# Seventy short moves in a pinned issue order: attention and early gate/up of a transformer block on one Trainium2 core

## The chip, the cores and the metric

The kernel runs on one core of one Trainium2 chip. The metric is the device time of one execution in microseconds, as a median over several executions. A core has five engines that run side by side, each through its own list of instructions in the order in which they were issued: PE (matrix unit), DVE (vector), ACT (scalar), POOL (GpSimd) and SP, which here only issues DMA transfers. They wait for each other by semaphores.

## The reference

A pre-norm block: linear attention, then a gated feed-forward layer, with 2048 tokens and width 1024.

```python
# x (1, 2048, 1024), wqkv (1024, 3072), wo (1024, 1024); 32 heads of 32; F = 3584
q, k, v = split(layernorm(x) @ wqkv)
phi = lambda t: where(t > 0, t + 1, exp(t)) + 1e-6
kv = einsum("bhsd,bhse->bhde", phi(k), v);  z = sum over s of phi(k)
o = (phi(q) @ kv) / (phi(q) . z + 1e-6)
h = x + o @ wo
n = layernorm(h)
gate = n @ W_gate;  gate = gate * (gate > 0);  up = n @ W_up
h2 = h + (gate * up) @ W_down
```

## The kernel before

Its large products run by the seven-product scheme of Strassen in Winograd's form: DVE forms sums of blocks of both operands, PE makes seven products of half the size instead of eight, and the results are combined in PSUM banks and by copies. Three banks matter: A (two of them), D (one) and E (two).

```python
def strassen(pool, work, mm, fin, sbufs=3, late=False, copies={}):
    ...
    def snap(v, nm, bank=A):              # a partial sum is copied out of its bank by ACT (L203)
        ...
        copies[nm, v] = nc.scalar.copy(out=snaps[nm, v], in_=bank[v][:])

    def m2(v):
        d = pool.tile([P, NW], FP32, tag="D", bufs=1, name="Dq")
        mm(d, 2, v, True)
        fin(0, 0, v, d, snaps["m1", v])
    for v in range(2):                    # product 1 -> A
        A[v] = pool.tile([P, NW], FP32, tag="A", bufs=2, name="Aq")
        mm(A[v], 1, v, True)
        snap(v, "m1")
    yield
    m2(0)                                 # product 2 -> D
    for v in range(2):
        mm(A[v], 6, v, False)             # product 6 on top of A
        snap(v, "u2")
    m2(1)
    yield
    for v in range(2):                    # product 5 -> E
        E[v] = pool.tile([P, NW], FP32, tag="E", bufs=2, name="Eq")
        mm(E[v], 5, v, True)
    ...
    for v in range(2):
        mm(A[v], 7, v, False)
        snap(v, "u3")
        fin(1, 1, v, E[v], snaps["u3", v])
    yield
    for v in range(2):
        mm(A[v], 4, v, False)
        fin(1, 0, v, A[v], None)
    yield
    for v in range(2):
        mm(E[v], 3, v, False)             # waits until fin(1, 1) has read E
        fin(0, 1, v, E[v], snaps["u2", v])
```

For the keys, `fin` is `phi_begin`: on DVE it adds the copied sum to the bank (L260, into `wo_mem`), on ACT where there is nothing to add (L258). `phi_end` follows when both halves are there: an exponential on ACT (L265), then L266 and L267 on DVE. For the values, `fin` is L424 on DVE or L422 on ACT.

```python
def left_sums(T, S, cols, eng):                                    # sums of the token side, per unit of tokens
    ...
    eng.tensor_tensor(out=s1, in0=a21, in1=a22, op=ALU.add)        # L166
    eng.tensor_tensor(out=s2, in0=s1, in1=a11, op=ALU.subtract)    # L167
    eng.tensor_tensor(out=a21.bitcast(FP16), in0=a11, in1=a21, op=ALU.subtract)   # L168
    eng.tensor_tensor(out=s4, in0=a12, in1=s2, op=ALU.subtract)    # L169
...                                                                # right_ops: the same for weights, L182 to L185
```

The tokens reach `left_sums` by a DMA transpose: statistics on DVE (L321, L323), two tiny ACT operations (L326, L327), one tiny DVE operation (L336), the normalization `xn` on ACT (L337), then `dma_start_transpose` into `xT` (L339). The query weights `wq_sb` are loaded while the keys are computed (L295). Units of four token tiles follow each other: keys of unit u, key-value products of unit u - 1 (`kv_ps`, L432), values of unit u.

After the queries (L503) the attention of each token tile runs in stages that are spread over steps: `nd` (products with `kvz`, L576; their reciprocals on ACT, L580 and L582; the division on DVE, L583), a DMA transpose, `wo_h` (the products `attn`, L606; the residual on DVE, L609; the second layer norm on ACT, L623 to L627), another transpose. `nd` and some `attn` products share a ring of three banks. The first gate/up products (L787) are mixed with them, with weight sums (L691, L695 to L697), additions (L796) and products (L801) on DVE.

The order of all these is not left to the scheduler. Numbers in the source say, engine by engine, which instruction follows which:

```python
ISSUE_ORDER = {
    "PE": """
        0*24 32*4 40*3 24*4 36*4 ...
    """,
    "DVE": """ ... """, "Activation": """ ... """, "SP": """ ... """, "Pool": """ ... """,
}
...
    for engine, words in ISSUE_ORDER.items():
        seq = []
        for word in words.split():
            start, length = (word.split("*") + ["1"])[:2]
            seq += emitted[engine][int(start):int(start) + int(length)]
        ...
        for late, first in zip(seq[1:], seq):
            tc.add_manual_dep(late, first.name, ..., reason="order")
```

`75*3` means: the three instructions from number 75 on, counted in the order in which the source emits them. The numbers end where the main gate/up loop begins (L914, at about 287 us); from there on the order is that of the source.

Of the kernel before, what the change touches and what calls it, by code (L numbers as in the profile page):

```python
# [19 lines left out]
def _load_act_set(nc, set_name="natural_log_exp_and_others"):  # L20
# [11 lines left out]

ISSUE_ORDER = {
    "PE": """
        0*24 32*4 40*3 24*4 36*4 28*4 43*5 56*12 48*4 68*4 52*4 80*4 88*4 72*4 84*4 92*3 76*4 95*121 232 216*16 233*44
        288*2 277*7 290*4 284*4 294*305 600*12 599 612*8 624 620*4 625*115 744*4 740*4 748*10 760*4 776*4 764*4 780*5
        788 758*2 785 768 786*2 769*5 789*3 816 774*2 817*2 792*3 819 795*3 820 798*2 821*3 848*5 800*16 824*6 853*3
        830*2 856*2 832*16 858*14 888*8 920*8 872*8 952*3 880*8 896*6 955*3 902*2 958*5 904*16 928*6 963*3 934*2 966*2
        936*16 968*12 984*8 980*4 1016*3 992*22 1019*3 1014*2 1022*38 1064*5 1060*4 1069*6 1080 1088*4 1075*5 1081*7
        1092*12 1112*2 1104*3 1114*4 1107*3 1118 1110*2 1119*13 1152*4 1132*4 1168*4 1156*4 1172*3 1160*3 1136*16  # L40
        1163*5 1175*5 1200*9 1180*4 1209*4 1184*16 1213*19 1248*19 1232*16 1267*21 1304*8 1288*16 1312*160
    """,
    "DVE": """
        0*6 7*3 6 10 58 11 16*2 12 18 13 19 25*3 59 28 20 14*2 21 61 23*2 29 22 34*2 30 36 31*2 37 42*2 33 44 46 45 47
        38*3 48 50 41 49 51 60 52 62 53 63 68 64 69 72 65 70 73 78 74 79 71 54 80 55*3 75 92 106 93 81 66 94 107 112
        108 113 95 114 98 109 76*2 67 99 115 100 116*3 86 82*2 122 84 89 119 85 123 96 124 87*2 90*2 125 166*2 97 169
        102*2 101 168 104*2 170 138 110 171 139*3 111 172 120 173 121 130 126*2 133 128*2 131*2 134*4 142*8 154 150
        157 151*3 155*2 158*8 174*15 192 189 193 190*2 194 196 195 197*5 206 202*2 207 204 210*2 216 208*2 205 212*4
        217 220*2 218 222 219 232 223*5 233 228*2 234 230*2 235 244 238 245 236*2 239 241 240 246*2 242*2 248 260
        249*6 261 255 257 256 262 258*2 263*2 268 265 269 266 271 270 267 272*4 277 276 280*2 278*2 283*3 282 288 291  # L50
        286 289 287 290 292*8 306*4 303 300*2 304 302 305 310 320 324 313 311*2 314 316*2 315 321*2 326 318 325 328
        319 323 327 329*2 334 356*3 331 360 332*2 335 361*2 336 363 343 337 344 387 389 338 359 345 340 339 388 341
        346 342 391 347*2 392 349 390 393*2 364 350*6 365*3 373 368*2 374 370 375 383*2 371 385 372 386 416 376 417
        377 418 378 419*2 379*2 421 381 422*2 401*2 382 403*2 395*4 412*4 399*2 405*7 424 427*4 425*2 431*7
    """,
    "Activation": """
        0*3 4*3 3 8 7 10*2 9 12 14 16*3 15 13 20 19 21*5 27*2 26 29*2 32*3 31 37*2 35 39 46 36 47*2 51 54 52 40 55 53
        41*2 59*2 43*2 56 45 61 49*2 78*2 57 83*2 58 80 62*4 85*3 68 66 69 88 67 71 91*2 70 93 72*6 81*2 89*2 94*41
        136 135 137*2 140 139 141*6 148 147 149*2 152 154 153 155 158 151 159 166 156*2 160 162 161 167 163*3 169*6
        168 191 180 182 181 183 175 192 176 184 177 185 178*2 193*2 186 195 187 197 188 198 189*2 196 199 201 200 202  # L60
        220 208*2 211 210 221 212*3 203 233 204*4 222*4 234 215*2 226 217 235 218 227 219 236 228 237 229 239 230 241
        231 240 232 242 238 243*2 250 252 251 253 245 254 246 255 247*3 256 262 257 264 258 263 259 261 265*3 260
        273*3 268*3 278 271*2 279*5 276*2 289*2 284 291*2 285 293*2 286*3 300 302 301 295 303 296 304 297 305 298*2
        312 311 313 306 325 307 314 308 315 327 316*2 309 318 310 326 319 328 320 329 321 330 322 332 323 341 324 342
        331 333*2 343*2 335 345 336*5 346*2 357 348*3 359 351 358 360 352*5 361 367*2 362 369*2 363 371 364*3 377 379
        372 378 373 380 374*3 381*3 385 384 386*2 389 388 390*2
    """,
    "SP": """
        0*9 10 12 14 16 18 9 20 11 22 13 26 15 28 17 30 19 32 21 36 23 27 40 29 24*2 31 33 44 34*2 37*3 42*2 41 46*3
# [1567 lines left out]
```

## Time and profile before

| | before |
|---|---|
| time, median of 3 runs | 734.84 us (733.66 to 735.07) |
| span of the profiled execution | 732.0 us, clock 1.000 |
| PE, DVE, ACT busy | 98%, 80%, 45% |
| PE, DVE, ACT busy in 40 to 60 us | 19.19, 18.38, 16.59 of 20 us |
| the same in 60 to 80 us | 17.27, 16.57, 9.41 |
| the same in 160 to 180 us | 19.24, 13.60, 16.39 |
| the same in 240 to 260 us | 19.56, 15.13, 11.19 |
| PE busy in 80 to 140 us, per 20 us | 19.89, 19.89, 19.89 |

The page gives the busy time of each engine over the whole span, the windows give it for a stretch. The waits view lists for each engine who ended its idle time; the timeline lists instructions in order of time. Ends of matmuls are modelled, so that a PE that looks busy may still hide small gaps; the spacing of starts tells them. A line number stands for a line of the kernel above (L260 is the line of `phi_begin` on DVE).

### The profile page before, as it was taken

Reading aid. Unit: us, or ns where it says so; the run is one execution under the profiler, and the core shown is the slowest. Engines: PE = TensorE matmul, PEld = TensorE weight load, DVE = VectorE, ACT = ScalarE, POOL = GpSimd, SP = SyncE. Lnnn points to the kernel's source line nnn. Section 1 sums busy time; section 2 is a strip of 40 time slices with the busy share of each in tenths; the row PEclk is TensorE's granted clock in tenths of the full one; section 3 lists DMA queues with packets and bytes.
Section 4 is the critical chain, followed back from the end, with each engine's and each line's share of the span. In section 5 each row is a group of like instructions: output and inputs, shape, how many; then the busy total and the mean of one; then the engine's idle time right before and its main releaser. Section 6 shows DMA issues by size and latency. Waiting matters only on the chain.

```text
span 732.0 us, 10580 instructions
## 1 busy us (share of the span) xinstructions
PE 716.7 (98%) x3947; PEld 380.3 (52%) x4000; DVE 583.1 (80%) x1039; ACT 325.8 (45%) x580; POOL 21.0 (3%) x56
## 2 busy tenths in 40 slices
PE   8998999999999999999999999999999999999997
PEld 3443555444444444444444444444444468888667
DVE  6998744686799777789998998988987379996677
ACT  4786554778897654434444444444444120000000
POOL 1000000000000000000000000000000001100210
PEclk9999999999999999999999999999999999999999
DMA  9766001169986524187457576565553499977932
GB/s 318 158 143 172 1 1 54 62 140 221 236 181 172 136 78 133 43 243 224 160 168 226 202 238 222 172 202 172 192 177 118 148 394 323 323 255 271 258 45 58
DMA packets 144708, 128.89 MB, mean 176 GB/s; under 512 B 50960, under 2 KB 127888, under 8 KB 144656
## 3 DMA queue, kind: packets, MB, share of 16 engines
q1 hardware_dynamic: 137584, 123.30, 55.5%
q0 software_dynamic: 5312, 3.15, 3.6%
q10 hardware_dynamic: 1760, 1.77, 0.7%
q8 instruction: 31, 0.51, 0.3%
q14 instruction: 21, 0.17, 0.1%
HBM read 76.81 MB, written 39.85 MB: 159 GB/s over the span
## 4 chain that ended last, share of the span: by engine, by line
PE 85%; ACT 6%; DVE 5%; DMA 2%; issue 2%; SPq 0%; DVEq 0%; ACTq 0%
PE accA L914 21%; PE accA L1408 8%; PE attn L606 6%; PE accX L914 6%; PE accY L914 5%; PE Aq L363 4%; PE accA L1234 3%; PE Aq L787 3%; PE accX L1408 3%; PE Aq L503 3%; PE accY L1408 3%; PE accA L1002 2%; PE Eq L363 2%; PE vp L414 2%; PE Eq L787 2%; PE kp L396 2%
## 5 line engine op out<-in xcount | busy, mean ns | idle before, releaser
L919 ACT COPY snap<-accA 128x1024 f32<-128x1024 f32 x52 | 52.5, 1011 | 65.6 <-PE accA L914 65.5
L924 ACT ACTIVATE gu<-gu 128x512 bf16<-128x512 bf16 x72 | 45.5, 632 | 80.6 <-DVE gu L923 80.5
L914 PEld LDWEIGHTS <-tg 128*128 128x128 f16 x384 | 37.6, 98 | 45.5 <-issue 0.3
L914 PEld LDWEIGHTS <-tu 128*128 128x128 f16 x384 | 37.6, 98 | 45.3
L606 PE MATMUL attn<-wo_mem,oT 128*128 128x512 bf16 x247 | 58.1, 379 | 1.6 <-DVE o_sb L583 1.0
L914 PE MATMUL accA<-hn,tg 128*128 128x512 f16 (+1 forms) x192 | 49.3, 379 | 0.0
L914 PE MATMUL accA<-hn,tu 128*128 128x512 f16 (+1 forms) x192 | 49.3, 379 | 0.0
L203 ACT COPY u<-Aq 128x512 f32<-128x512 f32 x54 | 31.3, 581 | 37.8 <-PE Aq L363 21.1
L1408 PEld LDWEIGHTS <-x 128*128 128x128 f16 (+1 forms) x448 | 43.8, 98 | 5.5
L606 PEld LDWEIGHTS <-oT 128*128 128x128 bf16 x256 | 24.7, 98 | 30.6 <-issue 2.9
L923 DVE TENSOR_TENSOR gu<-accX,snap 128x1024 bf16<-128x1024 f32 x26 | 31.7, 1220 | 10.1 <-ACT snap L919 7.8
L923 DVE TENSOR_TENSOR gu<-accY,snap 128x1024 bf16<-128x1024 f32 x26 | 31.7, 1220 | 7.7 <-ACT snap L919 7.7
L914 PEld LDWEIGHTS <-wg 128*128 128x128 bf16 x208 | 20.3, 98 | 25.8 <-issue 1.4
L914 PEld LDWEIGHTS <-wu 128*128 128x128 bf16 x208 | 20.3, 98 | 24.5
L363 PEld LDWEIGHTS <-xT 128*128 128x128 bf16 (+1 forms) x192 | 18.6, 98 | 24.8 <-issue 3.4
L1372 POOL DMA_DIRECT2D out_dram<-o x12 | 15.2, 1265 | 502.7 <-DVE o L1368 501.0
L583 DVE TENSOR_TENSOR o_sb<-nd,rd 128x384 bf16<-128x384 f32 (+1 forms) x48 | 23.7, 510 | 6.8 <-ACT rd L582 5.5
L1408 PEld LDWEIGHTS <-xs 128*128 128x128 f16 x280 | 27.4, 98 | 3.2
L1414 DVE TENSOR_TENSOR snap<-accA,u 128x1024 f32<-128x1024 f32 x16 | 19.5, 1222 | 11.5 <-PE accA L1408 11.3
L609 DVE SCALAR_TENSOR_TENSOR x_res<-attn,x_res 128x512 bf16<-128x512 f32 x32 | 22.0, 687 | 8.1 <-PE attn L606 8.1
L927 DVE TENSOR_TENSOR hq<-gu 128x512 bf16<-128x512 bf16 x48 | 20.3, 423 | 10.0 <-ACT gu L924 9.8
L1234 PEld LDWEIGHTS <-x 128*128 128x128 bf16 (+1 forms) x168 | 16.4, 98 | 19.6
(268 smaller groups left out, 1512.0 us busy)
## 6 DMA issues: line engine op xcount, KB each, us to landing
x<-x_dram SPq DMA_DIRECT2D x17, 896.0 KB, 8.7
x_dram<-hq SPq DMA_DIRECT2D x28, 512.0 KB, 3.0
wg<-in_B_W_gate_dram SPq DMA_DIRECT2D x14, 512.0 KB, 4.5
wu<-in_B_W_up_dram SPq DMA_DIRECT2D x14, 512.0 KB, 5.9
x_dram<-hq SPq DMA_DIRECT2D x28, 256.0 KB, 2.4
wraw<-in_B_W_down_dram SPq DMA_DIRECT2D x14, 512.0 KB, 4.1
t_dram<-wt SPq DMA_DIRECT2D x21, 256.0 KB, 2.3
xd<-x_dram SPq DMA_DIRECT2D x6, 896.0 KB, 6.7
```

Source lines behind the costliest of these rows:

```text
L203: copies[nm, v] = nc.scalar.copy(out=snaps[nm, v], in_=bank[v][:])
L363: nc.tensor.matmul(ps[:], lhsT=left[m - 1][:, kc, r + v * P:r + (v + 1) * P], rhs=right[m - 1][:, kc, :], start=(start and kc == 0), stop= ...
L583: nc.vector.tensor_tensor(out=ov[:, c0:c0 + n], in0=ndv[:, :, 0:P].rearrange("p k (h e) -> p k h e", h=HPC), in1=rd[:, 0:n, :].unsqueeze(3 ...
L606: nc.tensor.matmul(ps[:], lhsT=st["oT"][:, c, :], rhs=wo_sb[:, c, j * NW:(j + 1) * NW], start=(c == 0), stop=(c == KC - 1))
L609: added[t, j] = nc.vector.scalar_tensor_tensor(out=h_sb[:, j * NW:(j + 1) * NW], in0=ps[:], scalar=1.0, in1=h_sb[:, j * NW:(j + 1) * NW], ...
L787: nc.tensor.matmul(ps[:], lhsT=w(v, m)[:, kc, :], rhs=left[m - 1][:, kc, :], start=(start and kc == 0), stop=(kc == KH - 1), skip_group_ch ...
L914: nc.tensor.matmul(ps[:, v, :], lhsT=w[v][n - 1][:, kc, :], rhs=left[n - 1][:, kc, :], start=(t is not None and kc == 0), stop=(kc == KH - ...
L919: nc.scalar.copy(out=st[nm][:], in_=halves(st["A"]))
L923: add(out=g[:], in0=halves(st[nm]), in1=st[base][:], op=ALU.add)
L924: nc.scalar.activation(out=g[:, 0, :], in_=g[:, 0, :], func=ACT.Relu)
L1234: nc.tensor.matmul(ps[:, t * NW:(t + 1) * NW], lhsT=x_tile(n, s, kh)[:, f, (t0 + t) * P:(t0 + t + 1) * P], rhs=w_tile(n, kh)[:, f, :], sta ...
L1408: nc.tensor.matmul(pv[:, tt, :], lhsT=left(m)[:, f, tt * P:(tt + 1) * P], rhs=right(m)[:, f, :], start=(t is not None and f == 0 and tt % ...
```

## The change

Three of the five lists of numbers are changed: PE, DVE and ACT. Nothing is added or removed, and all data, tiles, buffers and DMA issues are as before, the order of the DMA issues included. 70 instructions move: 15 matmuls, 37 DVE and 18 ACT instructions, most by a few places. The aim is that an instruction that waits for a late DMA landing no longer stands ahead of others whose data is ready.

The diff (two numbers at the start of a run are the place in the source's order; cut to the lines that the text speaks of):

```diff
     "PE": """
-        0*24 32*4 40*3 24*4 36*4 28*4 43*5 56*12 48*4 68*4 52*4 80*4 88*4 72*4 84*4 92*3 76*4 95*121 232 216*16 233*44
...
+        0*24 32*4 40*3 24*4 36*4 28*4 43*5 56*12 48*4 68*4 52*4 80*4 88*4 72*4 84*4 92*3 76*4 95*101 200*3 196*4
+        203*13 232 216*16 233*44 288*2 277*7 290*4 284*4 294*305 600*12 599 612*8 624 620*4 625*115 744*4 740*4 748*10
...
     "DVE": """
-        108 113 95 114 98 109 76*2 67 99 115 100 116*3 86 82*2 122 84 89 119 85 123 96 124 87*2 90*2 125 166*2 97 169
-        102*2 101 168 104*2 170 138 110 171 139*3 111 172 120 173 121 130 126*2 133 128*2 131*2 134*4 142*8 154 150
...
+        108 113*2 95 109 76 117 77 67 115*2 118 86 98 100 82*2 99 84 89 119 122 85 123 96 124 87*2 90*2 125 166*2 97
+        102*2 101 168*2 104*2 110 170*2 138 140 111 120 139 121 173 130 126*2 133 128*2 131*2 136 134*2 172 141 137
...
     "Activation": """
-        41*2 59*2 43*2 56 45 61 49*2 78*2 57 83*2 58 80 62*4 85*3 68 66 69 88 67 71 91*2 70 93 72*6 81*2 89*2 94*41
...
+        59 42 60 55 43 41 44*2 56 49*2 61 78*2 57 83*2 58 80 62*4 85*3 68 66 69 88 67 71 91*2 70 72*2 93 74*4 81*2
+        89*2 94*5 100 99 101*34 136 135 137*2 140 139 141*6 148 147 149*2 152 154 153 155 158 151 159 166 156*2 160
```

Written out for the stretch in which the keys of the third unit begin, the order of DVE is (tile numbers left out):

```
before                              after
L424 v_sb <- Eq, u2                 L424 v_sb <- Eq, u2
L424 v_sb <- Eq, u2                 L424 v_sb <- Eq, u2
L182 tq <- wq_sb                    L260 wo_mem <- Dq, m1   (v = 0)
L166 xS10 <- xT11                   L182 tq <- wq_sb
L260 wo_mem <- Dq, m1   (v = 0)     L183 tq <- wq_sb, tq
L183 tq <- wq_sb, tq                L166 xS10 <- xT11
L167 xS11 <- xS10, xT10             L168 xT11 <- xT10, xT11
L168 xT11 <- xT10, xT11             L260 wo_mem <- Dq, m1   (v = 1)
L169 xS12 <- xT10, xS11             L260 wo_mem <- Eq, u3   (v = 0)
L260 wo_mem <- Dq, m1   (v = 1)     L167 xS11 <- xS10, xT10
L184 wq_sb <- wq_sb                 L260 wo_mem <- Eq, u3   (v = 1)
L260 wo_mem <- Eq, u3   (v = 0)     L185 tq <- wq_sb, tq
L185 tq <- wq_sb, tq                ... (L184 and L169 some ten places later)
L260 wo_mem <- Eq, u3   (v = 1)
```

The other moves, by the time at which the instructions ran before: on DVE, small shifts in the statistics and exponential sums at 23 to 37 us; at 39 to 56 us L184 and L260 ahead of statistics, L183 behind them, and L166 to L168 of the next unit behind four L260; at 85 us one L424 ahead of L266; at 198 and 210 us one L167 and one L169 a few places later; at 226 to 230 and 272 to 277 us weight sums (L691, L696, L697) later; at 270 us L609 and L621 ahead of L166 to L169. On ACT, copies of values (L416) and statistics regrouped at 25 to 39 us; the copies L203 of the key unit ahead of the normalizations L337 at 40 to 43 us and at 61 us; one L203 ahead of the last L265 at 84 us; L265 ahead of L626 and L627 at 170 us, behind L582 and L626 at 185 us; L627 ahead of L582 at 203 us; a second-layer-norm chain ahead of one L203 at 263 us. On PE, one to three matmuls of one group put a few places earlier, between those of another, at 43, 196, 205, 211, 226, 262 and 274 us.

More of the change, by code (lines that the diff above doesn't have):

```diff
@@ L34 @@
     "PE": """
-        0*24 32*4 40*3 24*4 36*4 28*4 43*5 56*12 48*4 68*4 52*4 80*4 88*4 72*4 84*4 92*3 76*4 95*121 232 216*16 233*44
[L36 to L39, printed above, removed]
@@ L40 @@
-        1092*12 1112*2 1104*3 1114*4 1107*3 1118 1110*2 1119*13 1152*4 1132*4 1168*4 1156*4 1172*3 1160*3 1136*16
-        1163*5 1175*5 1200*9 1180*4 1209*4 1184*16 1213*19 1248*19 1232*16 1267*21 1304*8 1288*16 1312*160
+        0*24 32*4 40*3 24*4 36*4 28*4 43*5 56*12 48*4 68*4 52*4 80*4 88*4 72*4 84*4 92*3 76*4 95*101 200*3 196*4
+        203*13 232 216*16 233*44 288*2 277*7 290*4 284*4 294*305 600*12 599 612*8 624 620*4 625*115 744*4 740*4 748*10
+        760*4 776*4 764*4 780*5 788 758*2 785 768 786*2 769*5 789*3 816 774*2 817*2 792*3 819 795*3 820 798*2 821*3
@@ new lines @@
+        848*5 800*16 824*6 853*3 830*2 856*2 832*16 858*14 888*8 920*8 872*8 952*3 880*8 896*6 955*3 902*2 958*5
+        904*16 928*6 963*3 934*2 966*2 936*16 968*12 984*8 980*4 1016*3 992*18 1024 1010*4 1019*3 1014*2 1022*2
+        1025*35 1064*5 1060 1069*3 1061*3 1072*3 1080 1088*4 1075*5 1081*7 1092*15 1112*6 1107*3 1118 1110*2 1119*13
+        1152*4 1132*4 1168*4 1156*4 1172*3 1160*3 1136*16 1163*5 1175*5 1200*4 1180*3 1204*5 1183 1209*4 1184*16
+        1213*19 1248*19 1232*16 1267*21 1304*8 1288*16 1312*47 1368 1359*9 1369*48 1424*2 1417*7 1426*46
@@ L42 @@
     """,
     "DVE": """
-        0*6 7*3 6 10 58 11 16*2 12 18 13 19 25*3 59 28 20 14*2 21 61 23*2 29 22 34*2 30 36 31*2 37 42*2 33 44 46 45 47
-        38*3 48 50 41 49 51 60 52 62 53 63 68 64 69 72 65 70 73 78 74 79 71 54 80 55*3 75 92 106 93 81 66 94 107 112
-        108 113 95 114 98 109 76*2 67 99 115 100 116*3 86 82*2 122 84 89 119 85 123 96 124 87*2 90*2 125 166*2 97 169
-        102*2 101 168 104*2 170 138 110 171 139*3 111 172 120 173 121 130 126*2 133 128*2 131*2 134*4 142*8 154 150
@@ L48 @@
[L48 to L52, printed above, removed]
@@ L53 @@
-        346 342 391 347*2 392 349 390 393*2 364 350*6 365*3 373 368*2 374 370 375 383*2 371 385 372 386 416 376 417
-        377 418 378 419*2 379*2 421 381 422*2 401*2 382 403*2 395*4 412*4 399*2 405*7 424 427*4 425*2 431*7
+        0*6 7*3 6 10 58 11 16*2 12 18 13 19 25*3 59 28 20 14*2 21 61 23*2 29 22 34*2 30 36 31 37 42*2 32 44 33 45 47
+        46 38*3 48 41 49 51 50 52 60 53 63 62 68 64 69 72 65 70 73 78 74 79 71 80 54*4 75 92 94 66 106 81 107 112 93
+        108 113*2 95 109 76 117 77 67 115*2 118 86 98 100 82*2 99 84 89 119 122 85 123 96 124 87*2 90*2 125 166*2 97
@@ new lines @@
+        102*2 101 168*2 104*2 110 170*2 138 140 111 120 139 121 173 130 126*2 133 128*2 131*2 136 134*2 172 141 137
+        142*8 154 150 157 151*3 155*2 158*8 174*15 192 189 193 190*2 194 196 195 197*5 206 202*2 207 204 210*2 216
+        208*2 205 212*4 217 220*2 218 222 219 232 223*5 233 228*2 234 230*2 235 244 238 245 236*2 239 241 240 246*2
+        242*2 248 260 249*6 261 255 257 256 262 258*2 263*2 268 265 269 266 271 270 267 272*4 277 276 280 278*2 281
+        283*3 282 288 291 286 289 287 290 292*8 306*3 303 300*2 304 302 305 309*2 320 324 313 311*2 314 316*2 315
@@ L55 @@
+        321*2 326 318 325 328 319 323 327 329*2 334 356*3 331 360 332*2 335 361*2 336 343 337 344 389 338 359 387 345
+        340 339 388 341 346 342 391 347 363 348 392 349 390 393*2 364 350*6 365*3 373 368*2 374 370 375 383*2 371 385
+        372 386 416 376 417 377 418 378 419*2 379*2 421 381 422*2 401*2 382 403*2 395*6 412*4 405*7 424 427*4 425*2
+        431*7
     """,
     "Activation": """
-        0*3 4*3 3 8 7 10*2 9 12 14 16*3 15 13 20 19 21*5 27*2 26 29*2 32*3 31 37*2 35 39 46 36 47*2 51 54 52 40 55 53
@@ L58 @@
-        41*2 59*2 43*2 56 45 61 49*2 78*2 57 83*2 58 80 62*4 85*3 68 66 69 88 67 71 91*2 70 93 72*6 81*2 89*2 94*41
[L59 to L66, printed above, removed]
+        0*3 4*3 3 8 7 10*2 9 12 14 16*3 15 13 20 19 21*4 27*2 25 29 26 30 32*3 37*2 35 31 39 46 36 47*2 51*2 40 54 53
@@ new lines @@
+        59 42 60 55 43 41 44*2 56 49*2 61 78*2 57 83*2 58 80 62*4 85*3 68 66 69 88 67 71 91*2 70 72*2 93 74*4 81*2
+        89*2 94*5 100 99 101*34 136 135 137*2 140 139 141*6 148 147 149*2 152 154 153 155 158 151 159 166 156*2 160
+        162 161 167 163*3 169*6 168 191 180 182 181 183 175 192 176 184 177 185 178*2 193*2 186 195 187 197 188 198
+        196 189*2 199 201 200 202 220 208*2 211 210 221 212*3 203 233 204*4 222*4 234 215*2 226 217 227 218 235 219
+        236 228 237 229 239 230 241 231 240 232 242 238 243*2 250 252 251 253 245 254 246 255 247*3 256 262 257 264
@@ L67 @@
+        258 263 259 261 260 265*3 273*3 268*3 278 271*2 279*5 276*2 289*2 284 291*2 285 293*2 286*3 300 302 301 295
+        303 296 304 297 305 298*2 312 311 313 306 325 307 314 308 315 327 316*2 309 318 310 326 319 328 320 329 321
+        330 322 332 323 341 324 342 331 333*2 343*2 335 345 336*5 346*2 357 348*3 359 351 358 360 352*5 361 367*2 362
+        369*2 363*4 371 377 379 372 378 373 380 374*3 381*3 385 384 386*2 389 388 390*2
     """,
```

## The prediction

> **What bounds the kernel now.** I read the page's busy shares first, then what the matrix unit (PE) waits for, then the windows, then the timeline around each wait.
>
> ```profile
> PE 716.7 (98%) x3947; PEld 380.3 (52%) x4000; DVE 583.1 (80%) x1039; ACT 325.8 (45%) x580; POOL 21.0 (3%) x56
> ```
>
> ```profile
> PE Dq L363 <- DVE wo_mem L260: 2.3, 1, 2.3
> ...
> PE attn L606 <- DVE o_sb L583: 1.0, 2, 0.7
> PE Eq L363 <- DVE wo_mem L260: 0.6, 1, 0.6
> PE Aq L363 <- ACT u L203: 0.3, 1, 0.3
> ```
>
> PE is busy for 98% of a 732.0 us span, so it is idle for 732.0 - 716.7 = 15.3 us in all. A new order adds and removes no work: whatever it gains must come out of those 15.3 us, and only out of the part that lies in the reordered stages. The waits view (engine, tile, line, who released it; total, times, longest) says that one single wait, for the vector engine (DVE), is 2.3 us. By window, PE idle is 3.0 us in 0-20 us (start-up, whose order the change leaves alone), 0.8 in 40-60, 2.7 in 60-80, 0.8 in 160-180, 0.4 in 240-260 and 0.1 to 0.2 in most others up to 300. After 300 us the issue order is the same in both kernels.
>
> The timeline shows why the long wait exists (start, duration, engine, operation; in brackets the idle time before it):
>
> ```profile
> 68.23 1.03 PE L363 MATMUL Dq<-pq_mem,xT 128*128 128x512 bf16 x4
> ...
> 69.09 1.89 PE L363 MATMUL Aq<-pq_mem,xS 128*128 128x512 f16 x8
> ...
> 70.13 1.23 DVE L182 TENSOR_TENSOR tq<-wq_sb 128x2048 f16<-128x2048 bf16 x1 [2.73 <-DMA wq_sb<-in_A_wqkv_dram]
> ...
> 71.98 0.69 DVE L166 TENSOR_TENSOR xS<-xT 128x1024 f16<-128x1024 bf16 x1 [0.63 <-DMA xT<-xn]
> ...
> 72.59 0.69 DVE L260 SCALAR_TENSOR_TENSOR wo_mem<-Dq,m 128x512 bf16<-128x512 f32 x1
> ...
> 73.33 1.02 PE L363 MATMUL Dq<-pq_mem,xT 128*128 128x512 bf16 x4 [2.35 <-DVE wo_mem L260]
> ```
>
> The product D is finished at 69.2 and its bank (there is only one) could be emptied by L260 at once. But L260 stands on DVE behind L182, which waits for the query weights to land (70.1), and behind L166, which waits for a DMA transpose (72.0). The same pattern, smaller, is 23 us earlier:
>
> ```profile
> 48.70 0.69 DVE L166 TENSOR_TENSOR xS<-xT 128x1024 f16<-128x1024 bf16 x1 [1.52 <-DMA xT<-xn]
> ...
> 49.38 1.28 DVE L260 SCALAR_TENSOR_TENSOR wo_mem<-Eq,u 128x512 bf16<-128x512 f32 x2
> ...
> 50.12 1.89 PE L363 MATMUL Eq<-pq_mem,xS 128*128 128x512 bf16 x8 [0.64 <-DVE wo_mem L260]
> ```
>
> I size a stall by starts and not by the modelled ends. Back to back, 512-column matmuls start 216 ns apart (the chain has 37 of them in 7.99 us). Eight from 69.09 leave the next start at 69.09 + 8 x 0.216 = 70.82; it came at 73.33, so **2.51 us** were lost. In the same way 47.59 + 1.73 = 49.32 against 50.12: **0.80 us**.
>
> [...] L260 had its data at 69.2 and started at 72.59, right behind the two blocked instructions. That is the whole reason why an order can matter. [...] in the chain of waits the transposes issued at 43.66 and 67.26 take 4.95 and 4.63 us to land, while the issue record of the one at 41.72 lasts 1.23 us. So the landing, and not the record, is what the DVE order has to be laid around. [...]
>
> **The change, part by part.** [...] Only what falls on a PE stall counts.
>
> 1. First key unit on DVE, 39-56 us. The four sums of unit 2 (L166 to L168) go behind the L260 copies, and half of the weight sums move too. New order from 39.3, with durations of the timeline: L182 1.2, L184 1.2, L260 0.6, statistics of tokens 1.9, L183 1.2, 0.8 of statistics, L185 1.2, which brings L260 on E to about 47.5, when the copy it needs (L203, ending 47.46) is just there. It ends at 48.1 and the second at 49.3; PE wants them at 49.3 and 50.2. The stall of 0.80 goes: **-0.80**.
> 2. The scalar engine after it. In the old order ACT ran without a break from 50.65 to 64, and PE waited for its copies (L203) three times: 0.24 us at 57.5, 0.45 at 61.2, 0.09 at 62.8, by the spacing of weight loads and matmul starts. Its run began at 49.50 with a normalization that waited for a small DVE operation behind the same blocked L166. Freed, it starts some 1.05 us sooner while PE comes 0.8 sooner, so ACT gains 0.25 on PE: the first stall goes, the second stays, as PE then comes faster by what the first gave back. The normalization L337 that stood ahead of the u3 copies (1.24 us) moves behind them, which ends the third. **-0.3** of 0.78.
> 3. Second key unit, 66-81 us. L260 on D becomes the first in the group, at about 69.3, ending 69.9; PE wants the bank at 70.8. L182, L183, L166, L168 follow at 70.1, 71.3, 72.5 and 73.1, then L260 for the second D and at 75.0 L260 for E, which PE needs at 76.9. The stall of 2.51 goes, and one of 0.11 at 80.1 with it: **-2.62**.
> 4. What that brings up. PE then enters the second value unit 3.5 us sooner, but ACT still has four exponentials (L265, 1.15 us each) to do there, each gated by one of two buffers that DVE empties. One copy (L203) moves ahead of the last exponential, the second stays behind it: exponentials at 76.8, 78.6, 79.8 and 81.5 with copies at 80.9 and 82.65 put its end at 83.2, where PE would want it at 82.95. **+0.3**.
> 5. Attention, 145-220 us. Only one move meets a stall:
>
> ```profile
> 170.27 1.24 ACT L627 ACTIVATE hn<-x_res,sm 128x1024 bf16<-128x1024 bf16 x1
> ...
> 171.42 1.14 ACT L265 ACTIVATE e<-pq_mem,negb 128x1024 bf16<-128x1024 bf16 x1
> ...
> 172.59 0.43 DVE L266 TENSOR_SCALAR e<-e 128x1024 bf16<-128x1024 bf16 x1 [1.29 <-ACT e L265]
> ...
> 174.26 1.89 PE L606 MATMUL attn<-wo_mem,oT 128*128 128x512 bf16 x8 [0.65 <-DVE o_sb L583]
> ```
>
>    The exponential L265 moves ahead of L627. DVE, idle 1.29 us for it, does L266 and L267 while ACT runs L627, and L583 then waits only for its reciprocal (ready at about 173.1) instead of starting at 173.66: half a microsecond of the 0.82 lost there: **-0.5**. The reordering at 185-186 saves at most 0.1. At 203 the order is reversed (L627 ahead of the reciprocal), which delays L583 by about 1.1 us, but its banks are wanted at 208.4 and released near 206.3.
> 6. 220-287 us. DVE work is spread and a few matmuls are put between others as filler. The stalls that I find there (0.18 at 238.7, 0.56 at 247.7) come from reciprocals behind L627 on ACT, and that order is untouched: **0**.
>
> Sum: -0.80 - 0.30 - 2.62 + 0.30 - 0.50 - 0.10 = **-4.0 us**, of which I take 3.9 to pass through. From 300 us on PE is gapless but for one wait of 1.1 us (L914 for L923, near 334), so a start 4 us sooner ends 4 us sooner. 734.84 - 3.9 = **730.9 us**, 0.5% less.
>
> **The rivals.** *A new wait in place of the old.* The bank is free sooner, but ACT becomes the one that PE meets between 50 and 90 us (steps 2 and 4). For it: ACT is busy 16.6 of 20 us at 40-60. Against: only 9.4 at 60-80. If step 2 gives nothing and step 4 costs 1 us, the sum is 3.0 and the time about 731.9. *The landings set the pace anyway.* DMA engines are fully loaded at 160-200 us (share 1.00 and 1.10), and a PE that comes 3.5 us sooner could find transposed tiles not yet there. For it: the load. Against: no PE wait in the view is for a DMA. If it takes 2 us back: 733. *The filler moves and later DVE order remove more.* If all spacing losses at 145-250 (about 2.9 us) went instead of 0.6: 728.6. *A harmful move*, such as that at 203 us, costs over 4 us: the timings of step 5 speak against it.
>
> **Range and chances.** All outcomes but the last lie between 728.6 and 733; runs of the kernel before spread over 1.4 us. I take 728.8 to 733.2. Two per cent would be 14.7 us, nearly all PE idle time, most of it in stages not touched: faster by over 2% 0.01, within 2% 0.975, slower 0.015.
>
> **What would show it.** Step 1 and 3: the two waits of PE for L260 are gone from the waits view, PE busy in 60-80 rises from 17.27 to 19.5 or more, and L182 no longer has DVE idle for 2.7 us ahead of L260. Step 2 and 4: a PE wait for ACT's L203 near 59 or 79 us, 0.2 to 0.5 each. Step 5: the attention wait for L583 near 170 us falls from 0.65 to about 0.2. Span near 728. I am wrong if PE shows a new wait over 1 us before 290 us, or if the later part (the first L914 to the end) changes in length by over 0.5 us.

## The result, and the profile after

| | before | after |
|---|---|---|
| time, median (4 runs each, on one chip) | 734.39 us (733.66 to 735.07) | 729.18 us (728.99 to 730.98) |
| ratio | | 0.9935, 95% interval 0.9915 to 0.9954 |
| span of the profiled execution | 732.0 us | 727.5 us |

The change gains 0.65%. By the two spans it is 4.5 us; the 5.2 us between the two medians contain the scatter of the kernel before, whose 55 runs in a later comparison have a median of 733.34. All line numbers of the kernel after are two higher, since its lists of numbers take two more lines (L260 is L262, L203 is L205); in an experiment they are higher by zero or one.

The page of the kernel after, share of the span:

```profile
PE 719.0 (99%) x4000; PEld 380.4 (52%) x4000; DVE 583.2 (80%) x1039; ACT 325.2 (45%) x580; POOL 20.8 (3%) x56
```

PE idle has fallen from 15.3 us to 727.5 - 719.0 = 8.5 us. That is 6.8 us less, more than the 4.5 us of span: the page of before has 3947 matmul records and this one all 4000, and busy time counts only what is recorded. A busy sum is therefore not the measure for a gain of this size; starts of the same matmul are.

What PE waits for, in the kernel after (engine, tile and line, who released it; total us, times, longest), complete:

```profile
PE tp L350 <- DVE xT L351: 1.4, 1, 1.4
PE spin L451 <- DVE zero L448: 1.2, 1, 1.2
PE accY L916 <- DVE gu L925: 1.1, 1, 1.1
PE attn L608 <- DVE o_sb L585: 0.4, 1, 0.4
PE tp L350 <- ACT xT L351: 0.2, 1, 0.2
```

No wait for L262 (L260 of before) is left, and none for the copies of ACT (L205). What is left is start-up, the one wait of the main gate/up loop, and one attention wait of 0.4 us. The windows say the same (window; busy us and instructions of PE, its weight loads, DVE, ACT, POOL; granted clock, DMA share, GB/s):

```profile
40.00:60.00 20.00, 19.99 (x117) 10.04 (x116) 19.69 (x39) 17.98 (x30) 0.81 (x5) 1.00 0.58 103
60.00:80.00 20.00, 20.00 (x117) 10.10 (x117) 17.38 (x29) 11.47 (x16) 1.15 (x5) 1.00 0.52 145
160.00:180.00 20.00, 19.99 (x109) 9.64 (x108) 14.40 (x35) 17.34 (x41) 0.53 (x3) 1.00 1.04 241
```

PE is without a gap in all three windows, where it had 19.19, 17.27 and 19.24 us. The timeline of the kernel after shows the places that answer to those shown of before:

```profile
47.51 0.69 DVE L262 SCALAR_TENSOR_TENSOR wo_mem<-Eq,u 128x512 bf16<-128x512 f32 x1
...
48.24 1.24 ACT L339 ACTIVATE xn<-x_sb,sma 128x1024 bf16<-128x1024 bf16 x1
...
49.34 1.89 PE L365 MATMUL Eq<-pq_mem,xS 128*128 128x512 bf16 x8
...
68.00 0.69 DVE L262 SCALAR_TENSOR_TENSOR wo_mem<-Dq,m 128x512 bf16<-128x512 f32 x1 [1.73 <-PE Dq L365]
...
68.61 1.22 DVE L184 TENSOR_TENSOR tq<-wq_sb 128x2048 f16<-128x2048 bf16 x1
...
69.46 1.03 PE L365 MATMUL Dq<-pq_mem,xT 128*128 128x512 bf16 x4
...
167.28 1.24 ACT L629 ACTIVATE hn<-x_res,sm 128x1024 bf16<-128x1024 bf16 x1
...
168.97 0.56 DVE L585 TENSOR_TENSOR o_sb<-nd,rd 128x384 bf16<-128x384 f32 x1 [0.64 <-ACT rd L584]
...
169.58 1.89 PE L608 MATMUL attn<-wo_mem,oT 128*128 128x512 bf16 x8
```

At 68.00 the bank D is emptied as soon as PE has filled it, and only then does DVE take up the weight sum L184 (L182 of before). The second product in D starts at 69.46 with no idle time ahead of it. At 49.34 and 169.58 too PE starts without a bracket.

To see where the time came from, I took the start of the same matmul in the two traces, at places between the stalls. "Shift" is the start in a kernel minus that in the kernel before, less the same difference at a matmul of the first key unit at 22.28 us. It leaves the start-up out, which scatters by up to 1.7 us although its first instructions stand in the same order in all kernels (last section). The first rows are the kernels of this case, the others the experiments that follow.

| shift, us, at | 51.8 | 61.2 | 68.4 | 73.3 | 81.2 | 162.7 | 174.3 | 217.9 | end |
|---|---|---|---|---|---|---|---|---|---|
| after | -0.79 | -1.29 | -1.38 | -3.89 | -3.99 | -3.94 | -4.70 | -4.52 | -4.55 |
| dve_only | -0.80 | -1.30 | -1.10 | -3.62 | -3.71 | -3.68 | -3.69 | -3.56 | -3.61 |
| act_pe_only | 0.29 | 0.27 | 0.18 | -0.44 | -0.43 | -0.12 | -0.95 | -0.23 | -0.19 |
| one_move | -0.06 | -0.07 | -0.06 | -2.57 | -0.79 | -0.78 | -0.88 | -0.91 | -0.94 |
| after_undo | -0.80 | -1.30 | -1.39 | -1.48 | -1.57 | -1.40 | -2.31 | -2.14 | -2.17 |
| seg_c | 0.03 | 0.01 | 0.02 | -2.49 | -2.59 | -2.43 | -2.56 | -2.58 | -2.61 |
| early_before | 0.07 | 0.06 | 0.06 | -2.45 | -2.54 | -2.59 | -2.59 | -2.61 | -2.61 |
| early_after | -0.80 | -1.29 | -1.38 | -3.89 | -3.99 | -3.99 | -4.69 | -4.51 | -4.53 |
| attn_only | 0.00 | -0.01 | -0.01 | 0.25 | 1.84 | 1.95 | 1.11 | 1.24 | 1.21 |
| a_only | -0.79 | -1.29 | -1.03 | -1.08 | -1.08 | -1.02 | -1.15 | -1.18 | -1.22 |
| few_moves | -0.80 | -1.30 | -1.39 | -3.90 | -3.99 | -3.97 | -4.63 | -4.51 | -4.55 |
| best | -0.80 | -1.30 | -1.38 | -3.90 | -3.99 | -4.06 | -4.71 | -4.53 | -5.05 |

Columns are times of the kernel before. The step between 68.4 and 73.3 is the wait of the second product in D, that ahead of 51.8 the wait for E, that between 162.7 and 174.3 the attention wait. The start-up difference that is left out is +0.02 us for the kernel after, so its row is also the whole change.

### The profile page after: what moved, and what is told of

It reads as the page before. It is cut to its first block, busy times and chain, and to the rows that moved or that the text cites. A ratio compares the mean times of both kernels' runs of the same rounds, so it can differ in the third digit from the quotient of the medians.

```text
span 727.5 us, 10634 instructions
## 1 busy us (share of the span) xinstructions
PE 719.0 (99%) x4000; PEld 380.4 (52%) x4000; DVE 583.2 (80%) x1039; ACT 325.2 (45%) x580; POOL 20.8 (3%) x56
## 4 chain that ended last, share of the span: by engine, by line
PE 92%; DVE 4%; ACT 2%; DMA 1%; issue 0%; SPq 0%; DVEq 0%; ACTq 0%
PE accA L916 21%; PE accA L1410 8%; PE attn L608 7%; PE Aq L365 6%; PE accX L916 6%; PE accY L916 5%; PE accA L1236 3%; PE Aq L789 3%; PE Aq L505 3%; PE accX L1410 3%; PE Eq L365 3%; PE accY L1410 3%; PE accA L1004 2%; PE vp L416 2%; PE kp L398 2%; PE Eq L789 2%
## 5 line engine op out<-in xcount | busy, mean ns | idle before, releaser
L205 ACT COPY u<-Aq 128x512 f32<-128x512 f32 x54 | 31.4, 581 | 36.5 <-PE Aq L365 19.7
L585 DVE TENSOR_TENSOR o_sb<-nd,rd 128x384 bf16<-128x384 f32 (+1 forms) x48 | 23.7, 509 | 7.1 <-ACT rd L584 6.1
```

The lines of the kernel that those rows point to most:

```text
L585: nc.vector.tensor_tensor(out=ov[:, c0:c0 + n], in0=ndv[:, :, 0:P].rearrange("p k (h e) -> p k h e", h=HPC), in1=rd[:, 0:n, :].unsqueeze(3 ...
```

## The experiments

**Which engine's list does it.** Two kernels split the change: dve_only has the new list for DVE and the old ones for PE and ACT, act_pe_only the reverse.

```diff
 ISSUE_ORDER = {
     "PE":         before   |  after
     "DVE":        after    |  before
     "Activation": before   |  after
 }                 dve_only |  act_pe_only
```

> The vector engine's new order alone, PE and ACT in the old order. Theory (head of line on DVE): both stalls of PE behind L260 (0.80 us near 50, 2.51 us near 73) go, and ACT follows a little: 3.3 to 3.8 us less than before. Rival (the matmul and ACT moves do the work): under 1.5 us less. Rival (landings set the pace): the stalls shrink but come back at the next landing, about 1.5 us less.

> The new order on PE and ACT alone, DVE in the old order. Theory: the stall of 2.5 us near 73 and most of the 0.80 us near 50 stay, only the attention stall near 174 (0.82 us) shrinks: 0.5 to 1.2 us less than before. Rival (the matmul and ACT moves do the work): 3 us less or more.

Measured: dve_only 730.1 us (13 runs; ratio 0.9962, 0.9952 to 0.9973), act_pe_only 734.54 us (19 runs; ratio 1.0017, 1.0008 to 1.0026). By its trace act_pe_only is 1.66 us late at 22 us, and from there to the end it is 0.19 us faster than before. That start-up makes the 0.0017 is not shown: only one execution was profiled, and the 14 of its 19 runs with a mean granted clock of 0.999 or more still have a median of 734.26. Why those runs are 1 us longer stays open. One line of the waits of each, dve_only first:

```profile
PE attn L606 <- DVE o_sb L583: 1.0, 2, 0.6
```

```profile
PE Dq L364 <- DVE wo_mem L261: 1.7, 1, 1.7
```

DVE's list alone brings 3.61 of the 4.55 us. It leaves the attention wait, as step 5 said (that move is on ACT). The ACT and PE lists alone leave the wait for D (the 0.62 that act_pe_only wins there goes with landings that stand some 0.4 us sooner on the same footing). The two parts add up to 3.80, not 4.55: act_pe_only gains 0.83 in attention (-0.12 to -0.95) and gives 0.72 of it back by 217.9, where its waits show a product of `nd` that waits 0.5 us for L584. So some of the other ACT or PE moves cost time where DVE keeps its old order; few_moves below, with old PE and DVE orders in attention, doesn't lose it. Which moves they are was not tried.

**One move instead of seventy.** In the kernel before, only L260 on the first D goes ahead of L182; everything else stays.

```diff
 (DVE, near 70 us)
+L260 wo_mem <- Dq, m1   (v = 0)
 L182 tq <- wq_sb
 L166 xS10 <- xT11
-L260 wo_mem <- Dq, m1   (v = 0)
 L183 tq <- wq_sb, tq
```

> The kernel before with one DVE instruction moved by two places: L260 on the first D of the third key unit ahead of L182 and L166. Theory: PE loses nothing near 73 us, 2.5 us less than before, stall of 0.80 near 50 untouched. Rival (landings set the pace): the wait moves to the next bank, and 1.5 us or less is left.

Measured: 733.28 us (12 runs; ratio 1.0004, 0.999 to 1.0017). The expectation of 2.5 us failed. The table says how: -2.51 at D, as expected, then +1.78 by the end of the same group. By the trace 0.94 us is left at the end; the medians don't show it, and that profile is 1.52 us late from start-up (last section). The waits and the timeline of one_move:

```profile
PE Eq L363 <- DVE wo_mem L260: 2.1, 3, 0.8
```

```profile
72.28 1.03 PE L363 MATMUL Dq<-pq_mem,xT 128*128 128x512 bf16 x4
...
79.33 1.02 PE L363 MATMUL Eq<-pq_mem,xS 128*128 128x512 bf16 x3 [0.84 <-DVE wo_mem L260]
...
81.06 1.02 PE L363 MATMUL Eq<-pq_mem,xS 128*128 128x512 bf16 x4 [0.71 <-DVE wo_mem L260]
```

PE now comes to E 2.5 us sooner, but L260 on E still stands behind L167, L168, L169 and L184, some 3 us of DVE work. The old stall had hidden that. What is left at the end of the group, 0.73 us, is what the rival foresaw (the wait moves to the next bank), but its cause is not a landing in the main: of the DVE time between L260 on D (70.82) and L260 on E (78.59) only 0.65 us are a wait for one, at L166, and seg_c below keeps 2.6 us with the same loads. So the place of one instruction is not the cure: the whole group has to be laid out for a PE that comes 2.5 us sooner.

**The same group, complete.** The kernel before, with the new DVE order for this group alone: L260 on D first, L183 ahead of L166, L184 and L169 behind the last L260 (the stretch of the table in the section on the change), and one L424 ahead of the last L266 after it.

> The kernel before with the whole new DVE order of the second stretch alone (from L182 of the query weights to the first L424 of the next value unit, 23 instructions; L184 and L169 go to its end). Theory as mended by the one-move run (the wait moved from bank D to bank E because L184 and L169 also stood ahead of L260 on E): no PE wait for L260 between 66 and 82 us, 2.4 to 2.7 us less than before, measured from the first key product to the end. Rival (landings set the pace): 1 us or less.

Measured: 731.38 us (5 runs; ratio 0.9957, 0.9942 to 0.9972), shift -2.61 at the end. In its waits the one for D is gone and nothing takes its place; the others of before are untouched:

```profile
PE attn L606 <- DVE o_sb L583: 1.0, 2, 0.6
PE Eq L363 <- DVE wo_mem L260: 0.7, 1, 0.7
PE Aq L363 <- ACT u L203: 0.3, 1, 0.3
```

**Undo that one place in the kernel after.** L261 on the first D (L262 of after) is put back behind the weight sum and the blocked token sum; the other moves stay.

```diff
 (DVE, near 68 us)
-L262 wo_mem <- Dq, m1   (v = 0)
 L184 tq <- wq_sb
+L168 xS10 <- xT11
+L262 wo_mem <- Dq, m1   (v = 0)
 L185 tq <- wq_sb, tq
-L168 xS10 <- xT11
```

> The changed kernel with that one instruction put back behind L182 and L166. Theory: 2.3 to 2.6 us more than the changed kernel, so 2 to 3 us less than before, with a PE wait of 2.2 us or more for L260 near 72. Rival (many small moves share the gain): less than 1 us more than the changed kernel.

Measured: 732.03 us (20 runs; ratio 0.9986, 0.9975 to 0.9996). At 73.3 its shift is 2.41 us short of that of the kernel after, at the end 2.38. The wait is back, with its old size and name:

```profile
PE Dq L364 <- DVE wo_mem L261: 2.3, 1, 2.3
```

So this place is needed and, by one_move, not enough.

**The landing instead of the order.** If L260 stands behind late landings, an earlier landing must do the same as another order. The loads of the query weights are held until a tile of the keys is complete; here they wait for the third and fourth tile of the unit, which are complete before the first and second. One kernel is the one before with this edit, the other the one after with it.

```diff
-hold(wq_sb[0:1, 0, j * NW:j * NW + 1], pk[units[u][j]][0:1, 0:1])
+hold(wq_sb[0:1, 0, j * NW:j * NW + 1], pk[units[u][2 + j]][0:1, 0:1])
 load_w(wq_sb, j, 0)
```

> The kernel before, its old order untouched, but the load of the query weights is released by the first two finished key tiles of the unit (e of the second token half) in place of the last two, so that it starts some 4 us sooner and lands ahead of its use. Theory (the loss is DVE standing behind a late landing): the stall of 2.5 us near 73 goes without any move, 2.2 to 2.7 us less than before. Rival (DVE has too much work there): 1 us or less is won. Rival (transfers only change places and the transposes land later): no gain.

> The changed kernel with the same earlier load. Theory: the new order already does not depend on the landing, so within 0.3 us of the changed kernel (about 4.5 us less than before). Rival (the new order still pays for the landing): 1 us or more less than the changed kernel.

Measured: early_before 731.61 us (9 runs; ratio 0.9965, 0.9954 to 0.9977), early_after 729.18 us (4 runs; ratio 0.9932, 0.9915 to 0.9949). In early_before the two loads are issued at 58.39 and 59.77 us, in a profile that is 1.58 us late from start-up; in the kernel before at 60.52 and 61.92. On the same footing the issue is 3.7 us sooner. They land at 64.12 and 67.06 (before 65.78 and 70.00), and the transposes behind them on the queue at 68.14 and 68.93 (before 71.09 and 71.89). The timeline of early_before:

```profile
68.95 1.22 DVE L182 TENSOR_TENSOR tq<-wq_sb 128x2048 f16<-128x2048 bf16 x1
...
70.08 0.68 DVE L166 TENSOR_TENSOR xS<-xT 128x1024 f16<-128x1024 bf16 x1
...
71.00 0.69 DVE L260 SCALAR_TENSOR_TENSOR wo_mem<-Dq,m 128x512 bf16<-128x512 f32 x1 [0.24 <-PE Dq L363]
```

L182 and L166 now start without waiting, and it is L260 that waits for PE: in the old order, with no instruction moved, the stall of D is gone (-2.61 at the end, the same as by the order in seg_c). With the new order the early load adds nothing (-4.53 against -4.55). Two cures of one wait don't add up, and that the first works without any move shows that the cause of this stall is the landing in front of L260, not the order as such.

**The first stretch alone.** In the kernel before, the one L166 of the first key unit goes behind the two L260 on E.

```diff
 (DVE, near 48 us)
-L166 xS10 <- xT11
 L336 sma <- mv
 L260 wo_mem <- Eq, u3   (v = 0)
 L260 wo_mem <- Eq, u3   (v = 1)
+L166 xS10 <- xT11
 L260 wo_mem <- Dq, m1   (v = 1)
```

> The old order with one L166 of the first key unit put behind the two L260 copies on E and u3. Theory: the blocked L166 makes the stall of 0.80 near 50 us, and by its blockage the ACT waits after it; so 0.8 goes at 50 us and up to 0.3 more by 68 us, while the stall of 2.5 us at 73 stays. Rival: the stall is set by L260's own place behind L182 and L184, so that less than 0.3 goes.

Measured: 732.67 us (one run; profile 1.22 us faster from 22 us on). One move takes the 0.79 of step 1 and 0.50 of the ACT waits behind it; then, between 61.2 and 68.4, 0.26 is given back at a matmul that waits for the last L203, behind the normalization L337. In the kernel after, ACT's own move (L203 ahead of L337) keeps that from coming up.

**The attention move alone.** In the kernel before, L265 goes ahead of L626 and L627 on ACT at 170 us.

```diff
+L265 e <- pq_mem, negb
 L626 sm <- sm
 L627 hn <- x_res, sm
-L265 e <- pq_mem, negb
```

> The kernel before with one ACT instruction moved: the exponential L265 at 171 us ahead of L626 and L627. Theory: the PE stall at the attention product near 174 us (0.82 us by spacing) falls to 0.2 or less, 0.6 to 0.8 us less in the stretch from 166 to 183 us. Rival (the ring of three banks delays the next product instead): under 0.3 us.

Measured: 734.94 us, one run. The stretch from 162.7 to 174.3 us is 0.84 us shorter, of which some 0.15 is given back in the next 9 us; in the kernel after it is 0.76, with as much given back. The total is longer all the same, for a reason that has nothing to do with the move: +1.84 us lie at 68 to 81 us, ahead of it (last section).

**Thirteen moves.** The kernel before with the DVE order of the two key units (11 instructions, at 49 to 56 and 70 to 81 us) and two moves on ACT (L203 ahead of L337 at 61 us, L265 ahead of L627 at 170 us). PE's list and all else are old. The second DVE group is that of seg_c; the rest is:

```diff
 (DVE, near 49 us)
-L166 xS10 <- xT11
 L336 sma <- mv
 L260 wo_mem <- Eq, u3   (v = 0)
+L321 stats
 L260 wo_mem <- Eq, u3   (v = 1)
 L260 wo_mem <- Dq, m1   (v = 1)
-L167 xS11 <- xS10, xT10
 L336 sma <- mv
-L168 xT11 <- xT10, xT11
-L321 stats
 L321 stats
 L323 mv <- stats
 L260 wo_mem <- Eq, u2   (v = 0)
+L166 xS10 <- xT11
+L168 xT11 <- xT10, xT11
 L266 e <- e
 L267 wo_mem <- wo_mem, e
+L167 xS11 <- xS10, xT10
 (ACT, near 61 us)
+L203 u3 <- Aq   (both)
 L337 xn <- x_sb, sma
-L203 u3 <- Aq   (both)
 (ACT, near 170 us: as in attn_only)
```

> The old order with only 13 of the moves: the DVE order of the two key units (11 instructions, near 49-56 us and 70-81 us), and two moves on ACT (the copy ahead of the normalization near 61 us, the exponential ahead of L627 near 170 us); everything else, the matmuls included, as before. My theory: these are the whole of the gain, the other 60 or so moves are filler. Then the stalls at 50.1, 57.5, 61.2, 62.8, 73.3, 80.1 and 174.3 us go as they did in the changed kernel, and the last matmul comes 4.2 to 4.7 us earlier than before (the changed kernel: 4.5). Rival: the small moves of statistics and matmuls are needed so that DVE and ACT are in time; then 2.5 to 3.5 us at most, with a wait for L260 or L203 left near 50-62 us.

Measured: 729.12 us (5 runs; ratio 0.9936, 0.9923 to 0.995), shift -4.55 at the end: all of the gain of the kernel after, column by column. The attention wait is as after:

```profile
PE attn L606 <- DVE o_sb L583: 0.4, 1, 0.4
```

So the other moves, those of the matmuls and of the statistics among them, bring nothing here that can be seen.

**A version beyond both.** The kernel after, with ACT moves of the same kind at the places that step 6 named as untouched, and one reversal taken back.

```diff
 (ACT, at 237, 245 and 203 us; lines of this kernel)
+L583 rd (two of them)                       # were behind L628 and a copy
 L628 hn <- x_res, sm
...
+L581 den <- nd;  L583 rd <- den              # were behind L628
 L628 hn <- x_res, sm
...
+L583 rd;  L581 den;  L583 rd                 # were behind L628, as in the kernel after
 L628 hn <- x_res, sm
```

> The changed kernel with ACT moves that it did not make: at 245 us the den and the reciprocal of the first nd go ahead of the normalization L627 (L629 in the changed kernel), at 237 us two reciprocals likewise, and at 203 us the reciprocals stand ahead of L627 as in the kernel before. Theory: the remaining stalls near 243.2 (0.54), 234.1 (0.18) and 207.1 us (0.29) go, since in each the banks are held by an o_sb product that waits for its reciprocal behind 1.24 us of L627: the last matmul comes 0.7 to 1.0 us earlier than in the changed kernel. Rival: the later normalization delays its DMA transpose by 0.3 to 0.5 us, or the copies on ACT, and PE meets those instead: less than 0.3 us.

Measured: 728.67 us (5 runs; ratio 0.993, 0.9917 to 0.9942), shift -5.05, that is 0.5 us better than after; 0.7 to 1.0 had been expected. The stall at 243.2 us is gone and makes all of the gain. That at 234.1 goes too, but 0.14 us won there is lost again before the next one:

```profile
241.31 0.56 DVE L584 TENSOR_TENSOR o_sb<-nd,rd 128x384 bf16<-128x384 f32 x1 [1.30 <-ACT rd L583]
...
242.58 1.67 PE L607 MATMUL attn<-wo_mem,oT 128*128 128x512 bf16 x7
```

L584 runs 1.24 us sooner than in the kernel after, and `attn` starts without a wait. The third edit did nothing: the stall of 0.29 us at 207.0 is still there, so it is not L627's place on ACT that makes it. few_moves and dve_only don't have it, and act_pe_only loses 0.62 us there, so it comes with a move on PE or another one on ACT; which one was not tried. It costs nothing in the end, as a stall of 0.23 us at 215.7 goes with it.

## Why the prediction was right

Predicted 730.9 us, measured 729.18; the range of 728.8 to 733.2 held it. The sum was -4.0, of which 3.9 were taken; the trace gives -4.55. The miss of 1.7 us is 0.65 of steps (2 and 4 below), about 0.65 by which the medians differ from the traces, and 0.45 because the median of before, 734.84 in three runs, came out as 734.39 in four. The number lies closer to that of the rival of the filler moves (728.6) than to 730.9, and the range, drawn from a spread of 1.4 us (55 later runs spread over 4.4), held it by 0.4: the total alone would not tell the two apart, the shifts do. Step by step, from the shifts:

| step | predicted | measured | where it is read |
|---|---|---|---|
| 1, first key unit | -0.80 | -0.79 | after, ahead of 51.8; a_only the same |
| 2, ACT behind it | -0.30 | -0.59 | after, 51.8 to 68.4 |
| 3, second key unit | -2.62 | -2.61 | after, 68.4 to 81.2; seg_c -2.61 |
| 4, new wait for ACT | +0.30 | 0 | after, 81.2 to 162.7: +0.05 |
| 5, attention, with 185 us | -0.60 | -0.58 | after, 162.7 to 217.9 |
| 6, 220 to 287 us | 0 | -0.03 | after, 217.9 to the end |

Steps 1, 3, 5 and 6 came out to within 0.03 us. The cause that the prediction gave for steps 1 and 3, an instruction with its data ready behind one that waits for a landing, is shown by the order for both (a_only; seg_c and after_undo), and by the landing for step 3 alone (early_before). The prediction read the cure of step 3 as the place of L260 on D; one_move showed that the rest of the group is as much part of it, 1.78 us of 2.51. Its working did have this, since it timed L260 on E as well: 75.0 against 76.9 us. Measured are 73.73 and 75.50, or 75.1 and 76.9 on the clock of that working, which left out the 1.38 of steps 1 and 2.

In step 5 the total is right by luck, since its parts are not. The exponential brought 0.76 instead of 0.5: L585 (L583 of before) started at 168.97, that is at 172.91 on the clock of before, instead of 173.66, and PE found its bank free. The reordering at 185 us, put at 0.1, gave nothing, and some 0.15 came back in the 9 us behind the exponential.

**Step 2 was mis-sized.** The prediction let ACT start 1.05 us sooner, PE 0.8, and kept the second stall whole, "as PE then comes faster by what the first gave back". The normalization (L339 of after) started at 48.24 instead of 49.50, 1.26 us sooner, since nothing of the blocked group stood ahead of its small operation any more; the whole unbroken run of ACT moved with it (copy at 59.34 instead of 60.62, 1.28).

```profile
49.50 1.24 ACT L337 ACTIVATE xn<-x_sb,sma 128x1024 bf16<-128x1024 bf16 x1 [1.18 <-DVE sma L336]
...
60.62 0.57 ACT L203 COPY u<-Aq 128x512 f32<-128x512 f32 x1
```

```profile
59.34 0.57 ACT L205 COPY u<-Aq 128x512 f32<-128x512 f32 x1
```

(The first two lines are of before, the last of after.) Against PE's 0.79 that is a lead of 0.5, and the two first stalls gave just that: 0.24 whole and 0.26 of the second one's 0.45. The third went by ACT's own move, as predicted: dve_only and a_only, which lack it, lose 0.20 and 0.26 between 61.2 and 68.4, and after gains 0.09.

**Step 4 was too cautious.** The second copy was to end at 83.2 us where PE would want it at 82.95. In the trace it ran from 81.69 to 82.27, and PE took up the bank at 82.55, in the middle of its eight matmuls from 81.69:

```profile
80.64 1.15 ACT L267 ACTIVATE e<-wo_mem,negb 128x1024 bf16<-128x1024 bf16 x1
...
81.69 1.89 PE L365 MATMUL Aq<-tv,xS 128*128 128x512 f16 x8
81.69 0.58 ACT L205 COPY m<-Aq 128x512 f32<-128x512 f32 x1
```

By these times what failed is a mix of two clocks. PE had been moved by all of steps 1 to 3, put at 3.5 us (the terms add up to 3.72); the exponentials, worked out on from step 3, had not been moved by steps 1 and 2, although their inputs come from the same PE. With the 1.38 us of these steps added, the first, second and last measured exponentials (75.56, 77.31, 80.64) stand at 76.9, 78.7 and 82.0, near the 76.8, 78.6 and 81.5 of the working. The error of some 1.4 us was larger than the 0.25 that it was to decide.

The rivals: a new wait on ACT did not come in the whole change. In a_only, half of it, one did (0.26 us), and in one_move one for DVE; in seg_c neither. No landing set the pace: the PE that came 4.0 us sooner (at 81.2) found its tiles, and the waits show none for a DMA. The harmful move at 203 us did no harm; a stall of 0.29 us nearby is not its own (best). The rival that filler moves remove more was wrong in its cause: few_moves has the same shifts without them.

## What to carry to other kernels

Where the waits view names a vector operation as the releaser of PE and the timeline shows that operation without a wait of its own, look at what stands ahead of it on its engine: if that waits for a landing, try another order or an earlier load; here either alone was enough. Lay out the whole group for the earlier arrival of PE before moving one instruction, since the stall hid the next one (2.51 us won, 1.78 given back). And size such gains by the starts of the same matmul in two traces, less the start-up; medians of a few runs scatter by as much as the gain of one step.

## What the runs showed of the hardware beside this

**In four traces PE's granted clock was 0.50 for some 3.4 us after a wait.** The one of attn_only is why it came out slow. Its windows (columns as above; the third from the end is the granted clock):

```profile
72.00:74.00 2.00, 0.51 (x3) 0.27 (x3) 1.86 (x3) 0.00 (x0) 0.00 (x0) 1.00 0.24 93
74.00:75.00 1.00, 1.00 (x4) 0.31 (x3) 1.00 (x2) 0.00 (x0) 0.00 (x0) 0.50 0.07 16
75.00:76.00 1.00, 1.00 (x4) 0.31 (x3) 1.00 (x3) 0.00 (x0) 0.00 (x0) 0.50 0.00 0
76.00:77.00 1.00, 1.00 (x4) 0.42 (x3) 1.00 (x3) 0.00 (x0) 0.00 (x0) 0.50 0.00 0
77.00:78.00 1.00, 1.00 (x6) 0.36 (x4) 1.00 (x1) 0.00 (x0) 0.00 (x0) 0.80 0.00 0
```

After a wait of 2.61 us for D the clock was 0.50 for 3.4 us: PE looks fully busy, but its matmuls start 0.43 us apart (by their weight loads) instead of 0.216. The stretch from 73.3 to 81.2 us took 9.45 us instead of 7.86. In the trace of the kernel before, the same wait was 2.35 us and the clock stayed at 1.00. At start-up three traces show the same: in act_pe_only a wait of 2.98 us ended at 9.64, the clock was 0.50 from 10.85 to 14.27 us, and the run was 1.66 us late at 22 us; one_move (2.07 us, ending at 9.56) and early_before (2.9 us) lost 1.52 and 1.58 in the same way, while best waited 2.6 us there and lost nothing.

The length of the wait alone does not sort these runs: the half clock followed one of 2.07 us (one_move) and not those of 2.35 (before) and 2.6 (best). What decides it is not shown; no run was laid out to vary it.

In attn_only the wait of 2.61 us cost 1.59 us on top of its own length, while waits of 2.3 to 2.6 us in before, after_undo and best cost no more than their own length. A comparison of few runs can be off by 1.5 us for such a cause outside the change. The run lists fit: 11 of the 55 runs of the kernel before and 5 of the 12 of one_move have a mean granted clock of 0.998 or less, and their medians (735.16 and 734.39 us) are 1.9 and 1.7 us above those of the rest (733.24 and 732.65).

**A transpose landed late behind loads on its queue.** In the kernel before, the transpose issued at 62.39 us, right behind two loads of the query weights, landed at 71.09, 8.7 us later; the one issued at 67.26, with the second load still to land at 70.00, took 4.63. Those at 41.72, 50.77 and 55.42 us, with no load just ahead, took 3.0 to 3.1; that at 43.66, behind an `x_res` load issued at 43.04, took 4.95. With the loads 3.7 us sooner (early_before) the first of these, itself issued 1.87 us sooner, landed 2.95 us sooner by the clock of its trace, 4.5 us on the same footing. That the loads are the cause is not shown by itself, since the transposes moved with them.
